# A build-time plan with measured durations, a lock for the score banks, six PSUM banks without fixed roles, and an earlier place for the mixing factors

## The chip, the cores and the metric

The kernel runs on one core of one Trainium2 chip. The metric is the device time of one execution in microseconds (us); the median of three runs stands for a kernel. The core has five engines that run side by side, each in the order of its own list: TensorE (PE, matmuls, with weight loads shown apart as PEld), VectorE (DVE), ScalarE (ACT), GpSimd (POOL), and SyncE (SP), which here issues all DMA transfers. They wait for one another by semaphores.

## The reference

Eight batches, eight heads, 576 tokens, head size 64. Each head's output is the sum of two attentions: one over queries, keys and values averaged over groups of four tokens, repeated four times, and a local one in which a token sees those less than four places away. The heads side by side give x, 8 x 576 x 512, which a channel-mixing layer takes:

```
q_d, k_d, v_d = mean over groups of 4 tokens
out = repeat(softmax(q_d k_d' / 8) v_d, 4) + softmax(mask(q k' / 8)) v
x_prev = x shifted by one token
xk = mu_k * x + (1 - mu_k) * x_prev
xr = mu_r * x + (1 - mu_r) * x_prev
k = relu(xk @ w_k)          # 512 -> 1024
v = (k * k) @ w_v           # 1024 -> 512
return sigmoid(xr @ w_r) * v
```

The three weight matrices arrive as 64-bit floats, so the kernel has to turn them into 32-bit numbers by bit operations.

## The kernel before

**Attention** goes by pairs of heads, 32 pairs (n), four to a batch. A pair's work is: load q and k (`load_raw`, tile raw, a ring of four), v in groups (`load_v4`, tile v or v4, a ring of two) and v in windows (`load_windows`, vw); transpose q and k on DVE (`turn_q`, `turn_k`); average on POOL (`pool_q`, `pool_k`, `pool_v`, L363 and L364); scores on PE into ps_a, two PSUM banks with the tag att; softmax on DVE, ACT and POOL (`down_top`, `score_top`, `down_exp`, `score_sub` and so on, among them `down_norm`, L485); transposes of the probabilities on PE (`down_turn`, L497 to L499) with a copy on ACT (`down_copy`, L506) and a spread on ACT (`spread`, L444); products with v on PE (`av_pe`, L516 and L522, into two banks pv, in the profile ps_v); and the sum of both outputs on DVE into xt (`av_out`, L555). From pair 5 on, the scores of a pair and the products of the pair before it are one step of PE (`run_pe`).

**The layer** goes by 18 chunks (c) of 256 tokens. A chunk needs: the difference of neighbouring tokens (`diff`, L576), the mixes (`mix_part`, L587 on ACT or L591 on DVE, with the mixing factors muk and mur; `mix_add`, `mix_high`, L605, `mix_low`, L610), eight products `k_pe` (L618, 12 matmuls each into a bank ps_g), relu and square on ACT (`k_relu`, L623; `k_high`, L629 and L630), a remainder (`k_low`, L637, on DVE or POOL), two products `r_pe` (L649, into ps_r), a sigmoid (`gate`, L658), eight steps `v_pe` (L667, accumulating in two banks acc), the last product (`store_mul`, L671) and the store. Every number is split in a high and a low part, so each product is three matmuls. Chunks 0 and 1 need batch 0; chunk 2 is the first that needs batch 1.

**The weights**: twenty tiles of 128 x 512, k0 to k7, v0 to v7 and r0 to r3, in the order k0-k3, v0-v3, k4-k7, v4-v7, r0-r3. Each is loaded on SP (`fetch_weight`, L223), written into a PSUM bank by ACT (`weight_scale`, L228), worked on by DVE three times (`weight_shift`, L232; `weight_tail`, L236; `weight_sign`, L241, into an SBUF tile w32, a ring of three shared with the gates), and its high part is taken by ACT (`weight_high`, L249). The low part of the first eight comes from PE through the same bank (`weight_diff`, L255 and L256) and ACT (`weight_left`, L259), and that of the others from POOL (`weight_low`, L264). By `w_bank(i)` the bank is c0 or c1 by turns.

**PSUM** has eight banks. Two are att. The other six have roles: g, a ring of two, for ps_g (and, for the first four pairs, the transposed probabilities, and ps_r of chunk 0); acc0 and acc1 for the accumulators, for ps_r of the later chunks, and for the products of the first four pairs; c0 and c1 for the weights and for the products of the later pairs.

**The order** of all work is set when the program is built. `Plan.add` records each step with its engine, an assumed duration in us, a rank (a due time), what it reads and writes, the ring slots that it takes (`new=`) and, for a load, an assumed DMA time. `Plan.order` then plays all engines forward by those numbers. Each time it takes the step that can start first, and the lowest rank among those that could start on that engine at the same moment. `SLACK` stretches the durations of all engines but PE, `SYNC` is the delay from one engine to another, and `PORT` lengthens some DVE steps while POOL works. A ring's slots are given in the order in which they were asked for, except for the tags in `ANY`. The order that comes out is emitted engine by engine and kept at run time, whatever the real durations are.

Of the kernel before, what the change touches and what calls it, by code (L numbers as in the profile page):

```python
# [17 lines left out]
P = 128  # L18
# [26 lines left out]
class Plan:  # L45
# [6 lines left out]
    ANY = ("c0", "c1", "sig")  # L52
    PORT = 0.6
    SYNC = 0.2
    SLACK = 1.06
# [33 lines left out]
    def order(self):  # L89
# [9 lines left out]
        free = {}  # L99
        dma_free = 0.0  # L100
# [6 lines left out]
        def start_of(t):  # L107
            s = max(ready_at[t["id"]], free.get(t["eng"], 0.0))
            for tile, tag in t["new"]:

# [11 lines left out]
        while waiting:  # L122
# [14 lines left out]
            s = starts[best]  # L137
            for tile, tag in t["new"]:
                ring[tag] = ring[tag][1:] + [tile]
                turn[tag] += 1  # L140
# [8 lines left out]
            end[best] = e  # L149
            self.when[best] = (s, s + us, e)  # L150
# [12 lines left out]
def attention_moe(ctx: ExitStack, tc, q, k, v, mu_k, mu_r, w_k, w_v, w_r, band, ident, out):  # L163
# [62 lines left out]
    def weight_scale(i):  # L226
        shaped[i] = pp.tile([P, 512], F32, tag=w_bank(i), name="ps_w", bufs=1)
        nc.scalar.activation(shaped[i], raws[i][:, :, 1].bitcast(F32), AF.Copy, scale=2.0 ** -112)  # L228
# [258 lines left out]
    def down_turn(n):  # L487

        d = st[n]
        if n < NP:  # L490
            d["ps_t"] = [pp.tile([72, 288], F32, tag="g", name="ps_t") for _ in range(2)]
# [16 lines left out]
    def av_pe(n):  # L508
# [4 lines left out]
        pv = [pp.tile([P, 432], F32, tag=x, name="ps_v", bufs=1) for x in av_banks(n)]  # L513
# [159 lines left out]
    def store_out(c, t):  # L673
# [5 lines left out]
                     xkl=2, xrh=1, xrl=1, kk=2, kh=4, kl=4, sig=3, g=2, acc0=1, acc1=1, c0=1, c1=1, att=1))  # L679
# [16 lines left out]
    def pair_loads(n):  # L696
        R, R1 = at_run[n], after(n)
        for nm in "qk":
            add("SP", 2.0, R - 18, load_raw, n, nm, new=[(f"{nm}raw{n}", "raw")], dma=1.92)
        add("SP", 0.5, R1 - 18, load_v4, n, new=[(f"v4{n}", "v4")], dma=1.26)  # L700
        add("SP", 2.0, R1 - 17, load_windows, n, new=[(f"vw{n}", "vw")], dma=1.92)

    def pair_scores(n, part):
        R, R1 = at_run[n], after(n)
        i = n % 2
        if part == 0:
            add("DVE", 0.78, R - 9, turn_q, n, r=[f"qraw{n}"], w=[f"qT{i}"])
            if SPLIT <= n < SPLIT + 2:
                add("POOL", 0.5, R - 9, clear_plane, i, w=[f"kT{i}"])
            add("DVE", 0.78 if n < SPLIT else 1.53, R - 8.5, turn_k, n, r=[f"kraw{n}"], w=[f"kT{i}"])  # L710
            add("POOL", 1.2, R - 7, pool_q, n, r=[f"qT{i}"], w=[f"qd.{i}"])
            add("ACT", 0.42, R - 6, last_q, n, w=[f"qd.{i}"])
            add("POOL", 1.4 if n < SPLIT else 2.0, R - 6, pool_k, n, r=[f"kT{i}"], new=[(f"kd{n}", "kd")])
            add(*(("DVE", 1.0) if n < VDVE else ("POOL", 2.15)), R1 - 8, pool_v, n, r=[f"v4{n}"], new=[(f"vd{n}", "vd")])
        if part == 1:
            add("DVE", 0.8, R1 - 14, down_top, n, r=[f"ps{n}"], w=[f"mxd{n}"])
            add("DVE", 1.12, R1 - 13.5, score_top, n, r=[f"ps{n}"], new=[(f"sm{n}", "sm")])
            add("ACT", 1.8, R1 - 13, down_exp, n, r=[f"ps{n}", f"mxd{n}"], new=[(f"ad{n}", "ad")])
            if n >= PEM:
                add("POOL", 0.92, R1 - 12, score_sub, n, w=[f"sm{n}"])  # L720
# [209 lines left out]
```

## Time and profile before

| | |
|---|---|
| time, median of 3 runs | 714.82 us (713.87 to 715.29) |
| the profiled execution, its time | 714.58 us |
| the profiled execution, its span | 712.8 us |
| mean granted TensorE clock | 0.964 of full speed |
| DMA | 62.19 MB, mean 87 GB/s |

The span runs from the first to the last record of the profile; the time counts what lies around it, too. "Busy" counts the time in which an engine has an instruction under way; issuing a DMA is not counted as busy. A row of the timeline gives start, duration, engine, line, operation, output<-inputs, count, and in brackets the idle time just before with what ended it. A row of the groups gives count, busy us, mean ns, then the idle time before and its releasers. A row of the windows view gives, for a stretch of the span, its length, the busy us of PE, PEld, DVE, ACT and POOL with their counts (an engine without such work may be left out), then granted clock, DMA busy share and GB/s. A row of the chain of waits gives start, duration, and the work that the end of the span can be traced back to.

### The profile page before, as it was taken

The page shows a single profiled execution, that of the slowest core. Times are in us where ns is not written, and L with a number is a line of the kernel's source. Part 1 is how long each engine was busy: PE and PEld are TensorE (multiplying, and loading weights), DVE is VectorE, ACT ScalarE, POOL GpSimd, SP SyncE. Part 2 cuts the span into 40 slices and gives each one's busy share as a digit, 9 for nine tenths or more (in the row PEclk, how much of TensorE's full clock was granted, in tenths as well). Part 3 has the DMA queues.
Part 4 walks back from the last instruction along what each step waited for, and adds up shares of the span by engine and source line. Part 5 has one row for each costly group of instructions (what it writes and reads, how often), then busy time and mean ns, then how long its engine had stood idle before and what let it go on. Part 6 is the DMA issues. An engine that isn't in the chain of part 4 may idle for free.

```text
span 712.8 us, 18403 instructions
## 1 busy us (share of the span) xinstructions
PE 658.3 (92%) x7352; PEld 565.4 (79%) x7352; DVE 470.3 (66%) x855; ACT 438.7 (62%) x1095; POOL 300.2 (42%) x374
## 2 busy tenths in 40 slices
PE   3576768997999999999999999999999999999997
PEld 1353657785878888888888888888888888988986
DVE  3764999749766887588852797577867874464111
ACT  2544886665856857576665657676757675744442
POOL 5533689655554555444242265435554521000000
PEclk9677799997999999999999999999999999999999
DMA  7899886554435343424142173434351100000000
GB/s 144 175 207 269 205 144 99 103 98 111 95 63 124 74 103 74 102 49 90 48 107 52 40 136 74 103 73 95 65 120 40 53 2 32 1 30 30 0 31 30
DMA packets 221848, 62.19 MB, mean 87 GB/s; under 512 B 205122, under 2 KB 214594, under 8 KB 221762
## 3 DMA queue, kind: packets, MB, share of 16 engines
q1 hardware_dynamic: 221762, 61.01, 39.8%
q8 instruction: 58, 0.95, 0.6%
q14 instruction: 28, 0.23, 0.1%
HBM read 51.55 MB, written 9.44 MB: 86 GB/s over the span
## 4 chain that ended last, share of the span: by engine, by line
PE 76%; DVE 9%; SPq 6%; DMA 5%; ACT 1%; issue 1%; POOL 0%; DVEq 0%; ACTq 0%; POOLq 0%
PE ps_g L618 26%; PE acc L667 25%; PE ps_r L649 14%; SPq L276 4%; PE ps_v L522 3%; PE ps_a L390 3%; PE ps_v L516 2%; DMA muk<-in_moe_mu_k_dram 1%; DMA wk<-in_moe_w_k_dram 1%; DMA vw<-in_v_dram 1%; SPq L299 1%; DVE ps_w L236 1%; PE ps_a L457 1%; DMA qraw<-in_q_dram 1%; DVE ps_w L232 1%
## 5 line engine op out<-in xcount | busy, mean ns | idle before, releaser
L618 PE MATMUL ps_g<-xkh,wk 128*128 128x256 f32 x1152 | 229.8, 286 | 4.8 <-ACT kk L623 4.1
L618 PEld LDWEIGHTS ps_g<-xkh,wk 128*128 128x128 f32 x1152 | 187.5, 191 | 11.4 <-ACT kk L623 4.7
L667 PE MATMUL acc<-wv,kh 128*128 128x512 f32 x576 | 182.4, 398 | 0.0
L618 PE MATMUL ps_g<-xkl,wk 128*128 128x256 f32 x576 | 163.1, 283 | 1.3 <-DVE xkl L610 1.3
L637 DVE TENSOR_TENSOR kl<-kk,kh 128x256 fp32r<-128x256 f32 x119 | 66.6, 561 | 108.6 <-ACT kh L630 100.6
L623 ACT ACTIVATE kk<-ps_g 128x256 f32<-128x256 f32 x144 | 54.9, 382 | 105.6 <-PE ps_g L618 102.0
L667 PE MATMUL acc<-wv,kl 128*128 128x512 f32 x288 | 113.6, 394 | 3.3 <-POOL kl L637 3.3
L667 PEld LDWEIGHTS acc<-wv,kh 128*128 128x128 f32 x576 | 102.1, 190 | 17.0 <-issue 0.2
L618 PEld LDWEIGHTS ps_g<-xkl,wk 128*128 128x128 f32 x576 | 110.4, 192 | 5.0 <-DVE xkl L610 1.6
L649 PE MATMUL ps_r<-wr,xrh 128*128 128x512 f32 x288 | 89.9, 393 | 0.5 <-DVE sig L671 0.2
L667 PEld LDWEIGHTS acc<-wv,kl 128*128 128x128 f32 x288 | 54.5, 189 | 17.1 <-POOL kl L637 4.8
L418 POOL TENSOR_TENSOR sm<-sm,mx 128x384 f32<-128x384 f32 x28 | 28.7, 1025 | 83.6 <-DVE mx L413 72.2
L630 ACT ACTIVATE kh<-kk 128x256 fp32r<-128x256 f32 x144 | 60.2, 418 | 4.6
L629 ACT ACTIVATE kk<-kk 128x256 f32<-128x256 f32 x144 | 60.1, 418 | 4.4
L637 POOL TENSOR_TENSOR kl<-kk,kh 128x256 fp32r<-128x256 f32 x25 | 20.5, 820 | 99.4 <-PE acc L667 81.4
L649 PEld LDWEIGHTS ps_r<-wr,xrh 128*128 128x128 f32 x288 | 52.3, 188 | 10.8 <-DVE sig L671 0.6
L464 DVE TENSOR_REDUCE mxd<-ps_a 128x3 f32<-128x432 f32 x32 | 19.4, 605 | 61.1 <-PE ps_a L390 54.2
L649 PE MATMUL ps_r<-wr,xrl 128*128 128x512 f32 x144 | 56.2, 390 | 0.0
L474 ACT ACTIVATE ad<-ps_a,mxd 128x144 f32<-128x144 f32 x96 | 35.4, 378 | 32.2 <-DVE mxd L465 12.1
L363 POOL TENSOR_TENSOR v<-v 72x512 f32<-72x512 f32 x32 | 45.5, 1421 | 20.7 <-DMA v<-in_v_dram 20.6
L364 POOL TENSOR_TENSOR vd<-v 72x256 f32<-72x256 f32 x32 | 24.3, 759 | 65.8 <-PE ps_v L516 64.5
L354 POOL TENSOR_TENSOR tk<-kz 64x288 f32<-64x288 f32 (+1 forms) x56 | 43.1, 771 | 10.6 <-DVE kz L327 5.4
(103 smaller groups left out, 1174.0 us busy)
## 6 DMA issues: line engine op xcount, KB each, us to landing
vw<-in_v_dram SPq DMA_DIRECT2D x126, 96.0 KB
qraw<-in_q_dram SPq DMA_DIRECT2D x128, 72.0 KB
kraw<-in_k_dram SPq DMA_DIRECT2D x128, 72.0 KB
v<-in_v_dram SPq DMA_DIRECT2D x32, 288.0 KB
out_dram<-sig SPq DMA_DIRECT2D x36, 256.0 KB
wk<-in_moe_w_k_dram SPq DMA_DIRECT2D x8, 512.0 KB
wv<-in_moe_w_v_dram SPq DMA_DIRECT2D x8, 512.0 KB
wr<-in_moe_w_r_dram SPq DMA_DIRECT2D x4, 512.0 KB
```

The source lines that it names most:

```text
L276: nc.sync.dma_start(raw[o:o + 32], src[b, 2 * p + e].rearrange("(c t) (g d) -> t c g d", t=32, g=2)[:, :, dh, :])
L354: nc.gpsimd.tensor_tensor(out=tk[h], in0=k4[:, :, 0:2], in1=k4[:, :, 2:4], op=ALU.add)
L363: eng.tensor_tensor(out=v4[:, :, 0:128], in0=v4[:, :, 0:128], in1=v4[:, :, 128:256], op=ALU.add)
L418: nc.gpsimd.tensor_tensor(out=s3, in0=s3, in1=mx[:, :, None].broadcast_to([P, 12, 32]), op=ALU.subtract)
L474: nc.scalar.activation(ad[:, t, :], ps[:, t, :], AF.Exp, scale=1.0 / 128, bias=mx[:, t:t + 1], accum_out=sd[:, t:t + 1])
L618: nc.tensor.matmul(ps, w_k_part(p, f, w), y[:, p, :], start=(m == 0), stop=(m == len(mm) - 1))
L623: nc.scalar.activation(kk, kq[c, f], AF.Relu)
L629: nc.scalar.activation(kk, kk, AF.Square)
L630: nc.scalar.activation(kh, kk, AF.Copy)
L637: eng.tensor_tensor(out=kl, in0=kk, in1=kh.bitcast(F32), op=ALU.subtract)
L649: nc.tensor.matmul(ps, y[:, p, P * t:P * t + P], ws[f"r{p}"][:, w, :], start=(m == 0), stop=(m == len(mm) - 1))
L667: nc.tensor.matmul(accs[c][t], x[:, P * t:P * t + P], ws[f"v{f}"][:, w, :], start=(f == 0 and m == 0), stop=(f == NF - 1 and m == 2))
```

## The change

No step of the computation is added or removed; its order, its PSUM banks and the plan's numbers are altered.

- The tags g, acc0, acc1, c0 and c1 go. Everything that used them asks for a "bank". `banks_for` gives one of six: among those whose last user has ended by the time at which the step could start, the ones freed latest; if there are too few, those that come free first. The chosen names b0 to b5 are kept in `plan.bank` and used as the tile's tag. att stays as it is.
- Three readers of a pair's score bank, `down_top`, `score_top` and `down_exp`, get a lock: in the plan, one starts only when the one before it has ended.
- The assumed durations are replaced; `SLACK` goes from 1.06 to 1.0, `SYNC` from 0.2 to 0.1, `PORT` from 0.6 to 0.8.
- `load_mus` goes from rank W0 = -25 to rank -88 and gets a DMA time of 0.8.

```
-    ANY = ("c0", "c1", "sig")
-    PORT = 0.6
-    SYNC = 0.2
-    SLACK = 1.06
+    ANY = ("sig",)
+    BANKS = 6
+    PORT = 0.8
+    SYNC = 0.1
+    SLACK = 1.0
...
+        def banks_for(t):
+            want = [tile for tile, tag in t["new"] if tag == "bank"]
+            if not want:
+                return 0.0, {}
+            s0 = max(ready_at[t["id"]], free.get(t["eng"], 0.0))
+            at = []
+            for k, old in enumerate(banks):
+                ends = [end.get(u) for u in self.tile_users[old]] if old is not None else []
+                if None not in ends:
+                    at.append((max(ends, default=-1.0) + self.SYNC, k))
+            if len(at) < len(want):
+                return None
+            late = sorted((x for x in at if x[0] <= s0), reverse=True)[:len(want)]
+            pick = late + sorted(x for x in at if x not in late)[:len(want) - len(late)]
+            return max(x[0] for x in pick), dict(zip(want, (k for _, k in pick)))
...
         def start_of(t):
-            s = max(ready_at[t["id"]], free.get(t["eng"], 0.0))
+            s = max(ready_at[t["id"]], free.get(t["eng"], 0.0), held.get(t["lock"], 0.0))
+            got = banks_for(t)
+            if got is None:
+                return None
+            s = max(s, got[0])
...
             end[best] = e
+            if t["lock"]:
+                held[t["lock"]] = e + self.SYNC
...
-        shaped[i] = pp.tile([P, 512], F32, tag=w_bank(i), name="ps_w", bufs=1)
+        shaped[i] = pp.tile([P, 512], F32, tag=plan.bank[f"ws{i}"], name="ps_w", bufs=1)
...
-        ps = pp.tile([P, CT], F32, tag="g", name="ps_g")
+        ps = pp.tile([P, CT], F32, tag=plan.bank[f"g{c}.{f}"], name="ps_g", bufs=1)
...
-            add("SP", 2.0, R - 18, load_raw, n, nm, new=[(f"{nm}raw{n}", "raw")], dma=1.92)
-        add("SP", 0.5, R1 - 18, load_v4, n, new=[(f"v4{n}", "v4")], dma=1.26)
-        add("SP", 2.0, R1 - 17, load_windows, n, new=[(f"vw{n}", "vw")], dma=1.92)
+            add("SP", 2.0, R - 18, load_raw, n, nm, new=[(f"{nm}raw{n}", "raw")], dma=2.4)
+        add("SP", 0.5, R1 - 18, load_v4, n, new=[(f"v4{n}", "v4")], dma=1.56)
+        add("SP", 2.0, R1 - 17, load_windows, n, new=[(f"vw{n}", "vw")], dma=2.5)
...
-            add("DVE", 0.8, R1 - 14, down_top, n, r=[f"ps{n}"], w=[f"mxd{n}"])
-            add("DVE", 1.12, R1 - 13.5, score_top, n, r=[f"ps{n}"], new=[(f"sm{n}", "sm")])
-            add("ACT", 1.8, R1 - 13, down_exp, n, r=[f"ps{n}", f"mxd{n}"], new=[(f"ad{n}", "ad")])
+            add("DVE", 0.8, R1 - 14, down_top, n, r=[f"ps{n}"], w=[f"mxd{n}"], lock=f"ps{n}")
+            add("DVE", 1.1, R1 - 13.5, score_top, n, r=[f"ps{n}"], new=[(f"sm{n}", "sm")], lock=f"ps{n}")
+            add("ACT", 1.2, R1 - 13, down_exp, n, r=[f"ps{n}", f"mxd{n}"], new=[(f"ad{n}", "ad")], lock=f"ps{n}")
...
         add("SP", 0.5, FETCH[i], fetch_weight, i, w=[base], dma=1.75)
-        add("ACT", 0.67, R, weight_scale, i, r=[base], new=[(f"ws{i}", w_bank(i))])
-        add("DVE", 0.6, R + 0.5, weight_shift, i, w=[f"ws{i}"])
+        add("ACT", 0.63, R, weight_scale, i, r=[base], new=[(f"ws{i}", "bank")])
+        add("DVE", 0.68, R + 0.5, weight_shift, i, w=[f"ws{i}"])
...
-        add("POOL", 2.2, -110, clear, w=["kT0", "kT1", "qT0", "qT1", "qd.0", "qd.1", "bd"])
-        add("SP", 1.0, W0, load_mus, w=["mu"])
+        add("POOL", 4.2, -110, clear, w=["kT0", "kT1", "qT0", "qT1", "qd.0", "qd.1", "bd"])
+        add("SP", 1.0, -88.0, load_mus, w=["mu"], dma=0.8)
```

More of the change, by code (lines that the diff above doesn't have):

```diff
@@ L99, in order @@
         free = {}
+        held = {}
+        banks, self.bank = [None] * self.BANKS, {}
+        def banks_for(t):
[13 more added lines that the diff above has]
+            return max(x[0] for x in pick), dict(zip(want, (k for _, k in pick)))
         dma_free = 0.0
@@ L137, in order @@
             s = starts[best]
+            for tile, k in banks_for(t)[1].items():
+                banks[k], self.bank[tile] = tile, f"b{k}"
             for tile, tag in t["new"]:
-                ring[tag] = ring[tag][1:] + [tile]
-                turn[tag] += 1
+                if tag != "bank":
+                    ring[tag] = ring[tag][1:] + [tile]
+                    turn[tag] += 1
             us = t["us"] * (1.0 if eng == "PE" else self.SLACK)
@@ L490, in down_turn @@
         if n < NP:
-            d["ps_t"] = [pp.tile([72, 288], F32, tag="g", name="ps_t") for _ in range(2)]
+            d["ps_t"] = [pp.tile([72, 288], F32, tag=plan.bank[f"pst{n}{kt}"], name="ps_t", bufs=1) for kt in range(2)]
         else:
@@ L512, in av_pe @@
         d = st[n]
-        pv = [pp.tile([P, 432], F32, tag=x, name="ps_v", bufs=1) for x in av_banks(n)]
+        pv = [pp.tile([P, 432], F32, tag=plan.bank[f"pv{n}{x}"], name="ps_v", bufs=1) for x in ("", "b")]
         for kt in range(2):
@@ L644, in r_pe @@
         xh, xl = xs[c, "xr"]
-        tag = r_bank(c, t)
-        ps = pp.tile([P, 512], F32, tag=tag, name="ps_r", bufs=2 if tag == "g" else 1)
+        ps = pp.tile([P, 512], F32, tag=plan.bank[f"r{c}.{t}"], name="ps_r", bufs=1)
         mm = [(y, w, p) for p in range(NP) for y, w in ((xh, 0), (xh, 1), (xl, 0))]
@@ L662, in v_pe @@
         if f == 0:
-            accs[c] = [pp.tile([P, 512], F32, tag=f"acc{t}", name=f"acc{t}", bufs=1) for t in range(2)]
+            accs[c] = [pp.tile([P, 512], F32, tag=plan.bank[f"acc{c}.{t}"], name=f"acc{t}", bufs=1) for t in range(2)]
         kh, kl = kq[c, f]
@@ L728, in pair_scores @@
+            add("DVE", 0.57, R1 - 6, score_turn, n, r=[f"sm{n}"], new=[(f"at{n}", "at")])
+            add("ACT", 0.95, R1 - 4, spread, n, r=[f"at{n}"], w=["bd"])
             add("PE", 0.65, R1 - 7, down_turn, n, r=[f"ad{n}"],
-                new=[(f"pst{n}{kt}", "g") for kt in range(2)] if n < NP else [(f"pst{n}0", "att")])
-            add("ACT", 0.85, R1 - 6, down_copy, n, r=[f"pst{n}0"] + ([f"pst{n}1"] if n < NP else []),
+                new=[(f"pst{n}{kt}", "bank") for kt in range(2)] if n < NP else [(f"pst{n}0", "att")])
@@ L807, in r_part @@
                 add("PE", 2.79, where[f"r{t}"], r_pe, c, t,
-                    r=[f"xrh{c}", f"xrl{c}"] + both(f"r{p}" for p in range(NP)), new=[(f"r{c}.{t}", r_bank(c, t))])
+                    r=[f"xrh{c}", f"xrl{c}"] + both(f"r{p}" for p in range(NP)), new=[(f"r{c}.{t}", "bank")])
             add("ACT", 3.8, where["r1"] - 3, gate, c, r=[f"r{c}.0", f"r{c}.1"],
@@ L814, in v_part @@
                 add("PE", 1.4, where[f"v{f}"], v_pe, c, f, r=[f"kh{c}.{f}", f"kl{c}.{f}"] + both([f"v{f}"]),
-                    new=[(f"acc{c}.{t}", f"acc{t}") for t in range(2)] if f == 0 else [],
+                    new=[(f"acc{c}.{t}", "bank") for t in range(2)] if f == 0 else [],
                     w=[f"acc{c}.{t}" for t in range(2)] if f else [])
```

74 lines of the change are left out of this document (34 added, 40 removed).

## The prediction

> **What bounds the kernel now.** I read the page first, for the share of each engine, and then the windows view, cut where the slices of the page change.
>
> ```profile
> span 712.8 us, 18403 instructions
> ...
> PE 658.3 (92%) x7352; PEld 565.4 (79%) x7352; DVE 470.3 (66%) x855; ACT 438.7 (62%) x1095; POOL 300.2 (42%) x374
> ```
>
> ```profile
> 10.00:74.00 64.00, 40.58 (x721) 25.95 (x721) 41.18 (x83) 31.38 (x84) 23.76 (x30) 0.74 0.95 206
> 74.00:128.00 54.00, 43.67 (x491) 36.73 (x492) 52.23 (x73) 39.72 (x100) 45.23 (x48) 0.92 0.76 148
> 128.00:175.00 47.00, 41.47 (x670) 34.07 (x672) 30.94 (x60) 30.34 (x79) 25.21 (x34) 0.92 0.50 102
> 175.00:210.00 35.00, 33.62 (x396) 29.50 (x392) 26.80 (x51) 23.31 (x58) 22.52 (x25) 0.96 0.42 81
> 210.00:709.00 499.00, 498.90 (x5099) 439.17 (x5089) 316.80 (x587) 311.94 (x772) 176.32 (x217) 1.00 0.28 63
> ```
>
> The profiled execution took 714.58 us, 1.8 more than its span of 712.8 and 0.2 below the median of 714.82, so no correction is needed. The windows rows (length, then busy time of PE, its weight loads, DVE, ACT, POOL, then clock and DMA) divide it into stages. From 210 to 709 PE is busy 498.90 of 499.00 us at a clock of 1.00. The same matmuls remain after the change, so here there is nothing to gain; the stage can only get worse. All that a better order can win lies before 210.
>
> From 10 to 74 the DMA engines are busy 0.95 of the time while four pairs of heads and sixteen of the twenty weight tiles come in. PE is busy 40.58 of 64.00 us at a clock of 0.74. DVE works only 41.18 us, so it idles 22.8. From 74 to 128 DVE is the bound: 52.23 of 54.00 us, 97%, while PE loses 10.33. From 128 to 175 PE loses 5.53 more, and 1.38 up to 210. PE idle from 74 to 210 is thus 10.33 + 5.53 + 1.38 = 17.2 us. That is the pool for an order that only fills PE, apart from an earlier start of chunk 0.
>
> What does DVE do in its full stage?
>
> ```profile
> 10.00:74.00 64.00, 14.72 (x24) 4.94 (x24) 17.11 (x26) 9.90 (x16) 0.74 0.95 206
> 74.00:128.00 54.00, 0.00 (x0) 0.00 (x0) 23.38 (x35) 7.42 (x12) 0.92 0.76 148
> ```
>
> ```profile
> L232 DVE TENSOR_SCALAR ps_w<-ps_w 128x512 int32<-128x512 int32 x20 | 13.7, 684 | 9.4 <-ACT ps_w L228 9.4
> L236 DVE SCALAR_TENSOR_TENSOR ps_w<-wk,ps_w 128x512 int32<-128x512 int32 x8 | 5.5, 689 | 0.2
> L241 DVE SCALAR_TENSOR_TENSOR w<-wk,ps_w 128x512 int32<-128x512 int32 x8 | 5.4, 674 | 0.2
> ```
>
> Instructions on the weight tile ps_w take 23.38 of those 52.23 us. One weight costs 0.684 + 0.689 + 0.674 = 2.05 us of DVE (shift, tail, sign), so about eleven and a half of the twenty conversions fall into the stage that DVE bounds, after a stage in which it idled 22.8 us. The ACT timeline (start, duration, what) shows why they come so late:
>
> ```profile
> 62.16 0.60 ACT L259 ACTIVATE wv<-ps_w 128x512 fp32r<-128x512 f32 x1 [0.87 <-PE ps_w L256]
> ...
> 63.18 0.63 ACT L228 ACTIVATE ps_w<-wv 128x512 f32<-128x512 f32 x1
> ...
> 64.94 0.60 ACT L259 ACTIVATE wv<-ps_w 128x512 fp32r<-128x512 f32 x1 [0.93 <-PE ps_w L256]
> ...
> 65.57 0.64 ACT L228 ACTIVATE ps_w<-wv 128x512 f32<-128x512 f32 x1
> ...
> 69.56 1.70 ACT L587 ACTIVATE xk<-dx,muk 128x256 f32<-128x256 f32 x4 [2.31 <-DMA muk<-in_moe_mu_k_dram]
> 71.17 0.57 ACT L259 ACTIVATE wv<-ps_w 128x512 fp32r<-128x512 f32 x1
> ...
> 72.17 0.62 ACT L228 ACTIVATE ps_w<-wk 128x512 f32<-128x512 f32 x1
> ...
> 75.27 0.57 ACT L259 ACTIVATE wv<-ps_w 128x512 fp32r<-128x512 f32 x1
> ...
> 76.20 0.65 ACT L228 ACTIVATE ps_w<-wk 128x512 f32<-128x512 f32 x1
> ```
>
> L228 begins a weight by writing its bank, c0 or c1 by turns; L259 is the last reader of that bank for the first eight weights. Four times a beginning (63.18, 65.57, 72.17, 76.20) follows the last read of the weight two before it (62.16, 64.94, 71.17, 75.27) within 1.1 us of its start. The last two are the fifth and sixth k tile. That their data had not just come, the chain of waits tells:
>
> ```profile
> 49.81 9.59 DMA wk<-in_moe_w_k_dram
> 59.42 10.05 DMA muk<-in_moe_mu_k_dram
> ```
>
> The first of the four later k tiles landed at 49.81 + 9.59 = 59.40, yet was begun at 72.17, 12.8 us later. The mixing factor, issued behind those k tiles and the last v tiles, landed at 69.47, so all eight were in by then (an inference from the order of issue).
>
> **The change, part by part.**
>
> *Six banks without roles.* It adds no instruction; it takes away the two-bank limit on weights, the two-bank ring of ps_g, and the sharing of acc between ps_r and the next accumulation. For weights the next limits are the landing and the ring of three w32 tiles. What room has DVE between 56 and 72?
>
> ```profile
> 59.35 0.58 DVE L438 STREAM_TRANSPOSE at<-sm 128x384 f32<-128x384 f32 x1 [3.39 <-POOL sm L433]
> ...
> 63.84 0.70 DVE L232 TENSOR_SCALAR ps_w<-ps_w 128x512 int32<-128x512 int32 x1 [2.61 <-ACT ps_w L228]
> ...
> 71.30 1.23 DVE L601 TENSOR_TENSOR xk<-xk,xt 128x1024 f32<-128x1024 f32 x1 [2.65 <-ACT xk L587]
> ```
>
> The idle times in brackets give 3.39 + 2.61 + 2.65 = 8.65 us; four weights need 4 x 2.05 = 8.2. So the four later k tiles fit there, beside waits for DMA and for pair 3. Taken out of the stage that DVE bounds at 97%, they bring the work behind them (turns, mixes and softmax of pairs 4 to 7, which chunk 2 needs) forward by up to 8.2 us, and PE has 17.2 us of idle time to give it back from. Bounds: nothing if the moved work meets another wait, and 17.2 if the whole pool goes. I take 8.2. The ring of ps_g itself has this row (whole waits in the stage, count, longest):
>
> ```profile
> PE ps_g L618 <- ACT kk L623: 4.1, 3, 1.7
> ```
>
> Its 4.1 us are part of the 17.2, not a sum beside it.
>
> *Mixing factors early.* Rank -25 becomes -88, which by the ranks puts both issues on SP ahead of the v tile of pair 1, the raw tiles of pairs 2 and 3 and everything up to the last v weight.
>
> ```profile
> 20.94 0.40 SPq L285 DMA_DIRECT2D v<-in_v_dram  x1
> ...
> 45.26 0.32 SPq L285 DMA_DIRECT2D v<-in_v_dram  x1
> ...
> 59.42 0.85 SPq L188 DMA_DIRECT2D muk<-in_moe_mu_k_dram  x1
> 61.21 0.37 SPq L189 DMA_DIRECT2D mur<-in_moe_mu_r_dram  x1
> 62.53 7.08 SPq L276 DMA_DIRECT2D qraw<-in_q_dram  x4
> ...
> 66.07 1.90 POOL L576 TENSOR_TENSOR dx<-xt 128x1024 f32<-128x1024 f32 x1 [6.76 <-DVE xt L555]
> ```
>
> The difference dx of chunk 0 ended at 66.07 + 1.90 = 67.97 and the first mix (L587, above) began at 69.56: 1.6 us go, if nothing else is late; next are the mixes themselves, in line on ACT. The price: the two issues hold SP 0.85 + 0.37 = 1.2 us, 3.1 with the gaps up to 62.53, and they are about 1024 packets of four bytes. The queue row prices a packet:
>
> ```profile
> q1 hardware_dynamic: 221762, 61.01, 39.8%
> ```
>
> 39.8% of 16 x 712.8 us over 221762 packets is 20.5 ns, so 1024 packets on 16 engines take about 1.3 us (estimate; the mean packet is 275 bytes, and smaller ones may be cheaper or dearer). DMA is full there, so v of pair 3, which POOL waits for, comes 1.3 us later (0 to 3.1). In return the raw tiles of pair 4 no longer stand behind them. Beside this row, the Trainium skill, DMA: Bandwidth & Descriptors (Measured), puts a small transfer at about 10.5 ns a packet and sets 512 B as the least for full rate (Specifications). By its price the 1.3 would be 0.7 us, an estimate; no row here isolates a four-byte packet.
>
> *Durations and lock.* They alter only the order. The lock keeps three readers of the score bank apart in the plan. The loads are re-rated from 1.92 to 2.4 us a raw tile, and so on. Adding the plan's own DMA terms up to v of pair 3 gives a planned landing near 45 us before (3 + 15.4 + 5.0 + 5.8 + 14 + 1.5) and near 52 after (3 + 19.2 + 6.2 + 7.5 + 14 + 0.8 + 1.5). The trace:
>
> ```profile
> 55.60 1.26 POOL L363 TENSOR_TENSOR v<-v 72x512 f32<-72x512 f32 x1 [6.58 <-DMA v<-in_v_dram]
> 56.94 0.72 POOL L364 TENSOR_TENSOR vd<-v 72x256 f32<-72x256 f32 x1
> 57.62 0.91 POOL L485 TENSOR_TENSOR ad<-ad,sd 128x432 f32<-128x432 f32 x1
> ...
> 58.58 0.43 PE L497 MATMUL ps_t<-idn,ad 128*72 128x128 f32 x1 [4.18 <-POOL ad L485]
> ...
> 62.70 0.91 PE L522 MATMUL ps_v<-bd,vw 64*64 64x48 f32 x48
> ...
> 73.82 0.58 PE L618 MATMUL ps_g<-xkh,wk 128*128 128x256 f32 x1 [0.70 <-ACT xkh L605]
> ```
>
> POOL stood 6.58 us at the head of its queue for v, with the normalisation of pair 3 (L485) behind it, and PE's transposes behind that. With L485 first, the sums behind it (vd ready at 57.66, against ps_v L522 at 62.70) could end up to 5.0 us earlier. With a plan still 3.4 us early the same order may stand, or a new one may wait as long elsewhere. Bounds -5.0 to +3.4; I take 0, since two of the three pool operations stay tied to that landing.
>
> *Less slack.* SLACK 1.06 becomes 1.0, SYNC 0.2 becomes 0.1, and a bank is picked as the latest freed before the start, with the least room. Where the plan is early by a little, PE now waits. PE falls behind the plan once and the others then have room, so I take 1.0 us; bounds 0 and 15 (one wait of the kind of L618 above, 4.1 / 3 = 1.4 us, in eleven of the chunks).
>
> Sum: 714.6 - 8.2 - 1.6 + 1.3 + 0 + 1.0 = 707.1, so 707 us.
>
> **Rivals.**
>
> 1. *The whole pool goes* (chance 0.15). If pairs 4 to 7 come early enough that chunk 2 never waits, all 17.2 us go, and the start gains 1.6 to 5: 714.6 - 17.2 - 1.6 = 695.8. For it: idle time of DVE in the first stage is 22.8 us, more than I use. Against it: DMA is at 0.95 there, and 0.76 even up to 128.
>
> 2. *A weight that has not landed stands at the head of ACT* (0.22), ending slower. Today the two banks hold weights back until long after landing. Without them the plan starts a weight where it believes its data to be. Its terms give a landing of the fifth k tile near 56.5 (52.2 + one vw of 2.5 + 1.75) against 59.40 in the trace, 2.9 us early. ACT and DVE are in order, so the exponentials, copies and spreads of pair 3 queue behind L228, and PE, POOL and chunk 0 behind those. Price: 3.4 us of start (the same error at v of pair 3) and 1.3 of packets, with none of the 8.2 recovered, because the DVE gaps of 59 to 72 then move with pair 3: 714.6 + 3.4 + 1.3 = 719.3. It decides once L228 of the fifth k tile stands on ACT ahead of L506 or L444 of pair 3. For it: in-order POOL already shows this very wait (6.58). Against it: later weights are planned nearly right.
>
> 3. *The steady stage loses what the start wins* (0.15): latest-freed banks and no slack cost PE about half a us in each of fourteen chunks, 7.5 in all: 707.1 + 7.5 - 1.0 = 713.6. Against it: PE idles 0.10 us in 499 with only two ps_g banks in turn. The Trainium skill, TensorE: The Clock Gate (A second HAM failure mode: psum-queue depth-cycling), says that cycling through PSUM banks can make PE idle briefly so often that its clock oscillates; the trace so far disagrees, with a clock of 1.00 in that stage. The rows give this a price too: at the 0.74 of the first stage, 20 us of steady work would take 27, again 7 us; no more of it is likely.
>
> **How the numbers follow.** My forecast, 707 with its own range of 701 to 712, has 0.48; the rivals 0.15, 0.22 and 0.15. A measurement of this kernel can tell about 0.2% (1.4 us) from no change. Faster: 0.48 + 0.15 + a third of rival 3 = 0.68. Same: half of rival 3, 0.08. Slower: 0.22 + the rest = 0.24. The range reaches from 696 (half of rival 1) to 719 (half of rival 2), leaving out about 0.17.
>
> **What would show it.** Right: L228 of the fifth k tile begins at 60 to 66, not 72.17; ps_w takes about 15 us of DVE after chunk 0 has begun, not 23.4; PE idle between 74 and 210 falls from 17 to 9; the first L618 starts within 2 us of 73.8; the window after 210 stays full. Wrong: ACT or DVE waits for a wk or v load of over 3 us between 45 and 70 with pair 3 behind it; PE waits for kk, pv or acc banks after 210; a clock under 1.00 there; or DVE just as full and the pairs as late, which would mean that the banks were not what held the weights back.

## The result, and the profile after

The changed kernel takes 706.69 us (median of 4 runs, 705.81 to 708.59), the kernel before 714.51 beside it (4 runs). The ratio is 0.9891 with a 95% interval of 0.9872 to 0.9911: 7.8 us less, where 7.8 was forecast (714.8 to 707.0).

The profiled execution took 708.59 us, the longest of the four, 1.9 above the median; its terms are therefore compared with one another more safely than with the median. First the head of the page, as for the kernel before:

```profile
span 706.7 us, 18406 instructions
...
PE 655.3 (93%) x7352; PEld 562.3 (80%) x7352; DVE 466.6 (66%) x855; ACT 438.9 (62%) x1095; POOL 303.1 (43%) x374
```

Then the windows view with the same stages:

```profile
10.00:74.00 64.00, 40.55 (x720) 26.73 (x720) 48.44 (x92) 35.96 (x92) 27.79 (x34) 0.74 0.95 208
74.00:128.00 54.00, 45.10 (x637) 38.94 (x638) 45.78 (x73) 35.46 (x95) 46.78 (x52) 0.90 0.90 156
128.00:175.00 47.00, 44.23 (x609) 37.81 (x608) 32.97 (x63) 36.23 (x92) 27.05 (x32) 1.00 0.52 107
175.00:210.00 35.00, 34.75 (x404) 29.69 (x403) 28.32 (x53) 21.91 (x56) 18.32 (x23) 1.00 0.42 92
210.00:702.00 492.00, 489.67 (x4985) 428.71 (x4984) 308.08 (x573) 307.31 (x758) 176.19 (x214) 1.00 0.30 62
```

The third number of a row after its length is DVE. It rises from 41.18 to 48.44 us in the first stage and falls from 52.23 to 45.78 in the second, so DVE is no longer the bound there. The idle time of PE is the length less the first number: 8.90, 2.77 and 0.25 us, together 11.9 from 74 to 210 in place of 17.2. After 210 it is 2.33, where it was 0.10.

The windows of the weight tile ps_w alone (PE, PEld, DVE, ACT), cut at the first matmul of chunk 0, show which work moved:

```profile
10.00:76.31 66.31, 13.83 (x24) 5.18 (x24) 26.31 (x39) 13.13 (x22) 0.73 0.95 212
76.31:128.00 51.69, 0.00 (x0) 0.00 (x0) 14.23 (x21) 3.71 (x6) 0.92 0.89 148
```

14.23 us of DVE work on weights are left behind that point; before it was 23.38 from 74 on. The ACT timeline shows the four later k tiles being begun:

```profile
62.57 0.63 ACT L258 ACTIVATE ps_w<-wk 128x512 f32<-128x512 f32 x1
...
64.14 0.62 ACT L258 ACTIVATE ps_w<-wk 128x512 f32<-128x512 f32 x1
...
64.87 0.61 ACT L258 ACTIVATE ps_w<-wk 128x512 f32<-128x512 f32 x1
...
66.50 0.62 ACT L258 ACTIVATE ps_w<-wk 128x512 f32<-128x512 f32 x1
```

L258 is the L228 of before. The fifth k tile begins at 62.57 instead of 72.17, and all four have begun by 66.50. But the start of chunk 0 did not come sooner. The DVE timeline up to it, and below it PE's:

```profile
71.69 0.69 DVE L271 SCALAR_TENSOR_TENSOR w<-wk,ps_w 128x512 int32<-128x512 int32 x1
72.29 1.74 DVE L625 TENSOR_TENSOR xk<-xk,xt 128x1024 f32<-128x1024 f32 x1
73.96 0.69 DVE L262 TENSOR_SCALAR ps_w<-ps_w 128x512 int32<-128x512 int32 x1
74.68 0.70 DVE L266 SCALAR_TENSOR_TENSOR ps_w<-wv,ps_w 128x512 int32<-128x512 int32 x1
75.48 0.69 DVE L271 SCALAR_TENSOR_TENSOR w<-wv,ps_w 128x512 int32<-128x512 int32 x1
76.08 1.22 DVE L634 TENSOR_TENSOR xkl<-xk,xkh 128x1024 fp32r<-128x1024 f32 x1
```

```profile
76.31 0.55 PE L642 MATMUL ps_g<-xkh,wk 128*128 128x256 f32 x1 [11.25 <-DVE w L271]
77.36 0.58 PE L642 MATMUL ps_g<-xkl,wk 128*128 128x256 f32 x1 [0.49 <-DVE xkl L634]
```

The sum of the mix (L625) stands in DVE's list behind a k weight's sign pass, and the low part of the mix (L634) behind three passes of a v weight. The first matmul waits for a bank which that v weight holds until L271 has read it (75.48 + 0.69 = 76.17). So it starts at 76.31, 2.5 us later than before.

The span can be taken apart into the start of the first `k_pe`, PE's idle time after it, and PE's busy time after it. The last is the page's PE total less the busy time up to that start, 658.3 - 40.4 before and 655.3 - 40.55 after.

| profiled execution | start of chunk 0 | PE idle after | PE busy after | span |
|---|---|---|---|---|
| before | 73.8 | 21.1 | 617.9 | 712.8 |
| changed | 76.3 | 15.7 | 614.7 | 706.7 |
| difference | +2.5 | -5.4 | -3.2 | -6.1 |

The -5.4 are -7.6 up to 210 us and +2.2 after it: from its own start of chunk 0 to 210, PE is idle 17.2 us before and 9.6 in the changed kernel. (The 11.9 above also hold the 2.3 us from 74 to the late start.)

The same matmuls are busy for 3.2 us less, and for a part of that time their clock is higher: from 128 to 175 us it is 1.00, where it was 0.92. That the clock accounts for all of it is not shown: old_margins, below, is busy 614.2 us after its start with a clock of 0.85 in that stage.

### The profile page after: what moved, and what is told of

Its sections match the earlier page's. It is cut to its first block, busy times and chain, and to the rows that moved or that the text cites. A ratio compares the mean times of both kernels' runs of the same rounds, so it can differ in the third digit from the quotient of the medians.

```text
span 706.7 us, 18406 instructions
## 1 busy us (share of the span) xinstructions
PE 655.3 (93%) x7352; PEld 562.3 (80%) x7352; DVE 466.6 (66%) x855; ACT 438.9 (62%) x1095; POOL 303.1 (43%) x374
## 4 chain that ended last, share of the span: by engine, by line
PE 73%; DVE 11%; POOL 5%; ACT 4%; issue 3%; SPq 2%; DMA 2%; DVEq 0%; POOLq 0%; ACTq 0%
PE ps_g L642 24%; PE acc L687 22%; PE ps_r L672 12%; PE ps_v L549 3%; PE ps_a L417 2%; PE ps_v L543 2%; SPq L303 1%; PE ps_a L477 1%; PE ps_a L484 1%; ACT L501 1%; ACT ad L501 1%; DVE mxd L491 1%; PE ps_a L422 1%; DVE kl L661 1%; PE ps_t L524 1%
## 5 line engine op out<-in xcount | busy, mean ns | idle before, releaser
L642 PE MATMUL ps_g<-xkh,wk 128*128 128x256 f32 x1152 | 230.1, 286 | 14.2 <-DVE w L271 11.9
L661 DVE TENSOR_TENSOR kl<-kk,kh 128x256 fp32r<-128x256 f32 x119 | 64.2, 540 | 118.0 <-ACT kh L654 110.8
L647 ACT ACTIVATE kk<-ps_g 128x256 f32<-128x256 f32 x144 | 54.5, 379 | 84.8 <-PE ps_g L642 79.1
L661 POOL TENSOR_TENSOR kl<-kk,kh 128x256 fp32r<-128x256 f32 x25 | 18.5, 740 | 125.0 <-PE acc L687 96.1
L445 POOL TENSOR_TENSOR sm<-sm,mx 128x384 f32<-128x384 f32 x28 | 24.3, 866 | 83.1 <-DVE sd L507 60.7
L390 POOL TENSOR_TENSOR v<-v 72x512 f32<-72x512 f32 x32 | 44.6, 1395 | 12.4 <-DMA v<-in_v_dram 12.3
L391 POOL TENSOR_TENSOR vd<-v 72x256 f32<-72x256 f32 x32 | 27.7, 866 | 51.0 <-PE ps_v L543 49.6
L381 POOL TENSOR_TENSOR tk<-kz 64x288 f32<-64x288 f32 (+1 forms) x56 | 40.9, 731 | 16.5 <-DVE kz L354 12.5
```

What stands on the lines that cost most here:

```text
L381: nc.gpsimd.tensor_tensor(out=tk[h], in0=k4[:, :, 0:2], in1=k4[:, :, 2:4], op=ALU.add)
L390: eng.tensor_tensor(out=v4[:, :, 0:128], in0=v4[:, :, 0:128], in1=v4[:, :, 128:256], op=ALU.add)
L391: eng.tensor_tensor(out=vd, in0=v4[:, :, 0:64], in1=v4[:, :, 64:128], op=ALU.add)
L642: nc.tensor.matmul(ps, w_k_part(p, f, w), y[:, p, :], start=(m == 0), stop=(m == len(mm) - 1))
L647: nc.scalar.activation(kk, kq[c, f], AF.Relu)
L661: eng.tensor_tensor(out=kl, in0=kk, in1=kh.bitcast(F32), op=ALU.subtract)
```

## The experiments

Twelve kernels, timed against the kernel before on the same chip. In each the result is the median; the ratio is to the kernel before. That kernel's medians beside them, 714.33 to 714.48 us, hardly differ, so medians of different groups of runs, on different chips, are compared here, too. Starts, idle times and busy times are those of the one profiled execution of a kernel. Where a plan's number or rule is edited the plan is made anew, and with it the order on all engines, except where the text says otherwise.

### One part alone, on the kernel before

**banks_only**: six banks with latest-freed choice; every number, margin and rank as before, no lock.

```
-    ANY = ("c0", "c1", "sig")
+    ANY = ("sig",)
+    BANKS = 6
...
+        def banks_for(t):
...
-        ps = pp.tile([P, CT], F32, tag="g", name="ps_g")
+        ps = pp.tile([P, CT], F32, tag=plan.bank[f"g{c}.{f}"], name="ps_g", bufs=1)
```

> Only the six banks without roles; the durations, SLACK, SYNC, PORT, no lock and the late mixing factors are those of before. Theory 1 (the banks win by letting weights be converted before chunk 0): 705 to 709 us, the scaling of the fifth k tile begins at 60 to 66 us as it does in the changed kernel (62.6) and not at 72.2, and PE is idle about 12 us between 74 and 210, not 17. Theory 2 (the measured durations win, the banks only go along): 713 to 716 us, with the old idle time of PE.

Measured: 715.69 us, 1.0014 [1.0002, 1.0026]. The part that was to bring 8.2 us brings nothing by itself. Its weights do move (the fifth k tile is begun at 62.10, as theory 1 asked), as the windows of ps_w show, cut at its own first `k_pe`:

```profile
10.00:83.18 73.18, 13.38 (x24) 5.29 (x24) 28.15 (x42) 15.94 (x26) 0.73 0.98 215
83.18:128.00 44.82, 0.00 (x0) 0.00 (x0) 12.25 (x18) 1.23 (x2) 0.90 0.79 129
```

Only 12.25 us of DVE work on weights are left behind that start. But the start itself is at 83.18, 9.4 us later than before. PE's idle time after it is 15.0 us (21.1 before), so the late start takes back what the fuller stage gives. The waits of PE between 74 and 210 (total, times, longest) list banks held by others at the top:

```profile
PE ps_g L642 <- DVE w L271: 5.4, 1, 5.4
PE ps_g L642 <- ACT sig L678: 3.9, 1, 3.9
```

**banks_oldest**: the same, but the bank that has been free longest.

```
-            late = sorted((x for x in at if x[0] <= s0), reverse=True)[:len(want)]
-            pick = late + sorted(x for x in at if x not in late)[:len(want) - len(late)]
+            pick = sorted(at)[:len(want)]
```

> The six banks alone, as in banks_only (old durations, margins and DMA times, no lock, late mixing factors), but a plan that takes the bank that has been free longest. Theory 1 (banks_only gained nothing because its late weights and chunk 0 wait for one another's banks: it lists 5.4 us behind the weights' DVE pass and 3.9 us behind the sigmoids): most of that goes, first k matmul before 78 us and 706 to 711 us. Theory 2 (it gained nothing because the old DMA times let the plan hand work to engines before its data has landed, and because early weights crowd chunk 0): first k matmul stays behind 80 us and the time stays at 712 to 717 us.

Measured: 713.69 us, 0.9992 [0.9979, 1.0006], first `k_pe` at 81.11. That is what theory 2 gave and not theory 1: six banks alone gain nothing that can be measured, and chunk 0 starts 7 to 9 us late under both rules of choice. The plan finds the same order on all five engines as for banks_only, so the two differ only in the banks: the wait of 5.4 us behind the weight's pass is gone, the one behind the sigmoids is still 3.3, chunk 0 starts 2.1 us sooner, and the median is 2.0 us lower, though the two intervals overlap. Which of theory 2's two grounds it is, the DMA times or the crowd of weights, this run doesn't tell.

**numbers_only**: durations, margins, DMA times and lock of the change; the roles of the banks and the rank of the mixing factors as before.

```
-    SLACK = 1.06
+    SLACK = 1.0
...
-            add("SP", 2.0, R - 18, load_raw, n, nm, new=[(f"{nm}raw{n}", "raw")], dma=1.92)
+            add("SP", 2.0, R - 18, load_raw, n, nm, new=[(f"{nm}raw{n}", "raw")], dma=2.4)
...
```

> Only the new durations, SLACK, SYNC, PORT and the lock, with the old roles of the banks and the late mixing factors. Theory 1: 713 to 717 us, the fifth k tile still begun at 70 us or later, because two banks hold it back. Theory 2: 705 to 709 us. If both parts are needed together, both this run and the one with the banks alone stay above 711.

Measured: 712.99 us, 0.9981 [0.9966, 0.9996]: 1.5 us less, at the edge of theory 1. Both this run and banks_only stay above 711, as the expectation said if both parts are needed together. But theory 1's reason is only half right. With two banks the fifth k tile is begun long before 70 us; the two behind it wait until 70.70:

```profile
62.06 0.65 ACT L231 ACTIVATE ps_w<-wk 128x512 f32<-128x512 f32 x1
...
70.70 1.16 ACT L231 ACTIVATE ps_w<-wk 128x512 f32<-128x512 f32 x2
```

**factors_only**: the kernel before with the mixing factors fetched early.

```
-        add("SP", 1.0, W0, load_mus, w=["mu"])
+        add("SP", 1.0, -88.0, load_mus, w=["mu"], dma=0.8)
```

> Only the mixing factors' rank and DMA time. The recorded working gave -1.6 us for the wait and +1.3 for the packets ahead of v of pair 3: 714 to 715, no change that can be told. A rival: the two issues cost SP so much that chunk 0 starts later: 716 to 718. Another: the wait was hiding a longer one and all later loads come 3 us earlier: 711 to 713.

Measured: 710.21 us, 0.9932 [0.9905, 0.9959]: 4.3 us less, with chunk 0 at 73.9, no earlier than before. That is outside all three ranges given, and its runs are far apart (706.64 to 712.03, the last being the profiled one). The gain is in PE's idle time after the start (17.6 us for 21.1), where the prediction had put none of it. Its cause stays open.

The three parts alone, +1.2, -1.5 and -4.3 us, make -4.6 together; the change makes -7.8. They don't add, but the 3.2 us between the two sums are less than the scatter of orders found below.

### One part undone, in the changed kernel

**factors_late**: the mixing factors at their old rank.

```
-        add("SP", 1.0, -88.0, load_mus, w=["mu"], dma=0.8)
+        add("SP", 1.0, W0, load_mus, w=["mu"])
```

> The changed kernel with the mixing factors back at their late rank and without a DMA time. If their place is worth nothing there, 706 to 708 us. If chunk 0 of the changed kernel would have to wait for them (they landed at 69.5 us before, and its first mix begins at 69.4 now), at most 1 us more: 706.5 to 708.5. If they are a pillar of the gain: 710 or more.

Measured: 706.79 us, 0.9886 [0.9859, 0.9913], against 0.9891 of the changed kernel. Inside the change the early fetch is worth nothing measurable. On PE, DVE, ACT and POOL the two plans differ in 17 places only, so this is nearly a comparison within one order.

**two_weight_banks**: at most two weights in PSUM at a time, the limit of before, by a ring of two that holds no memory.

```
...
-        add("ACT", 0.63, R, weight_scale, i, r=[base], new=[(f"ws{i}", "bank")])
+        add("ACT", 0.63, R, weight_scale, i, r=[base], new=[(f"ws{i}", "bank"), (f"wb{i}", "wb")])
...
```

> The changed kernel, with at most two weights at a time in PSUM, in any of the six banks, so that weights wait for the second weight before them as they did before the change. All else keeps its freedom. Theory 1 as recorded (weights converted early are what the banks win): 712 to 715 us, idle time of PE after its first layer product back from 16 to about 20 us. Theory 3, formed after the runs of the parts (early weights win idle time of PE later and lose it again at the start of chunk 0, which they delay by 2.5 us in the changed kernel and by 9.4 with the old durations): chunk 0 starts at 73 to 75 instead of 76.3 us, 2 us earlier, idle time after it is 4 us longer, so 708 to 711 us. If the weights do not matter at all: 705 to 708 us.

Measured: 709.85 us, 0.9942 [0.9929, 0.9955]: 3.2 us of the change are lost when weights may no longer run ahead, not 8.2. The time is in theory 3's range. Chunk 0 starts at 74.39, as it said, but PE's idle time after that is 17.3 us, 1.7 longer than the 15.6 of the changed kernel and not 4; its busy time is 618.0, 3.2 longer. From the start to 210 us PE is idle 10.8 us (changed 9.6, before 17.2). So under the two-bank limit, with another order, most of the fall in idle time is still there.

**old_margins**: `SLACK`, `SYNC` and `PORT` as before.

```
-    PORT = 0.8
-    SYNC = 0.1
-    SLACK = 1.0
+    PORT = 0.6
+    SYNC = 0.2
+    SLACK = 1.06
```

> The changed kernel with SLACK 1.06, SYNC 0.2 and PORT 0.6 as before. My term of +1.0 us for the smaller margins: 705 to 706 us, with the idle time after 210 us down from 2.3 to 0.1. Rival (the margins are part of a good start, since a slower plan orders other things first): chunk 0 at 79 us or later and 708 to 712 us.

Measured: 711.24 us, 0.996 [0.9944, 0.9976]: 4.5 us slower than the change. The number is the rival's, but its reason isn't: chunk 0 starts at 72.64, sooner than in the changed kernel. After 210 us the idle time does fall, to 0.85. The loss lies from 128 to 175 us:

```profile
128.00:175.00 47.00, 35.04 (x537) 29.95 (x536) 31.54 (x58) 24.75 (x63) 22.57 (x29) 0.85 0.41 89
```

PE is idle 11.96 us there (the changed kernel 2.77), for the most part behind POOL's normalisation (L512, 5.7 us) and a mix (6.0).

**old_dma_times**: DMA times of raw, v and vw as before.

```
-            add("SP", 2.0, R - 18, load_raw, n, nm, new=[(f"{nm}raw{n}", "raw")], dma=2.4)
+            add("SP", 2.0, R - 18, load_raw, n, nm, new=[(f"{nm}raw{n}", "raw")], dma=1.92)
...
```

> The changed kernel with the old DMA times of raw, v and vw tiles (1.92, 1.26, 1.92) in the plan. Theory 3 (the measured DMA times keep weights and pair 3 from being put at the head of a queue before their data is there): chunk 0 starts at 80 us or later, ACT or DVE stands over 3 us before a weight or behind v, 709 to 714 us. Rival (DMA times do not matter, the engine durations do): 705 to 708 us, start near 76 us.

Measured: 718.23 us, 1.0053 [1.0034, 1.0071]: 11.5 us slower than the change and slower than before, outside both ranges. Chunk 0 starts at 73.9, not at 80 or later, and from 45 to 76 us ACT's longest wait for a weight is 2.2. The wait that the prediction found on POOL is back, longer. POOL's waits from 10 to 76 us, then its timeline there, then that of the changed kernel:

```profile
POOL v L390 <- DMA v<-in_v_dram: 21.7, 4, 7.8
```

```profile
54.60 1.27 POOL L390 TENSOR_TENSOR v<-v 72x512 f32<-72x512 f32 x1 [7.85 <-DMA v<-in_v_dram]
55.95 0.73 POOL L391 TENSOR_TENSOR vd<-v 72x256 f32<-72x256 f32 x1
56.64 0.90 POOL L512 TENSOR_TENSOR ad<-ad,sd 128x432 f32<-128x432 f32 x1
```

```profile
56.64 0.91 POOL L512 TENSOR_TENSOR ad<-ad,sd 128x432 f32<-128x432 f32 x1 [8.87 <-DVE sd L508]
57.50 1.27 POOL L390 TENSOR_TENSOR v<-v 72x512 f32<-72x512 f32 x1
```

The re-rating does put the normalisation of pair 3 (L512, the L485 of before) ahead of the pooling of v (L390). Yet it begins at 56.64 in both: with the wait for v gone, it waits 8.87 us for its sums from DVE instead. So the 11.5 us do not come from this place; and with PE idle 21.8 us after a start of 73.9, and busy 617.9, its profiled execution is like that of the kernel before in every term of the table. That execution took 715.47 us, 2.8 below the median, so the profile holds only a part of the 11.5.

**no_lock**: without the lock.

```
...
-            add("ACT", 1.2, R1 - 13, down_exp, n, r=[f"ps{n}", f"mxd{n}"], new=[(f"ad{n}", "ad")], lock=f"ps{n}")
+            add("ACT", 1.2, R1 - 13, down_exp, n, r=[f"ps{n}", f"mxd{n}"], new=[(f"ad{n}", "ad")])
...
```

> The change without the lock alone. Theory 1 (the lock does nothing for the path, as the prediction had it; the readers of one score bank are in its order on DVE anyway): 705 to 709 us. Theory 2 (it keeps the exponential off the head of ACT's queue, where it would hold the conversions behind it): 710 to 714 us, with more idle of PE between 74 and 210 us than the 12.0 us of the changed kernel.

Measured: 717.53 us, 1.0049 [1.0031, 1.0066], outside what either theory gave. Theory 1 falls as a number; theory 2 has the direction, but little of the size: from 74 to 210 us PE is idle 13.6 us (the changed kernel 11.9), and from 45 to 76 us the exponential stands idle at the head of ACT once, for 1.55 us. Chunk 0 starts at 72.96, sooner than with the lock. From 210 to 702 us PE is idle 5.55 us (the changed kernel 2.33):

```profile
210.00:702.00 492.00, 486.45 (x4961) 424.68 (x4960) 307.16 (x572) 305.49 (x750) 173.90 (x212) 1.00 0.29 63
```

After its start PE is idle 23.4 us in all and busy 619.1 (changed 15.6 and 614.7). Why a plan without the lock comes out so is not shown.

### The same order, other banks

**oldest_bank**: the changed kernel with the bank that has been free longest, the edit shown under banks_oldest. Here the plan finds the same order of instructions on all five engines as for the changed kernel; only the bank behind a tile differs. With banks_only and banks_oldest it is one of the two pairs in this study that aren't also a comparison of two orders.

> The changed kernel, giving the bank that has been free longest instead of the one freed last. Theory (the first layer product waits 1.2 us for a bank that a weight still holds, and the 2.3 us of idle time of PE after 210 us are such waits): start of chunk 0 at about 75.1 us, under 0.5 us of idle time after 210, 703 to 705 us. Rival (the waits are for data, the bank only shows in the semaphore): 706 to 708 us, nothing moved.

Measured: 703.29 us (702.02 to 703.74), 0.9842 [0.983, 0.9855]; the interval does not touch that of the changed kernel. The choice of the latest-freed bank costs 3.4 us. PE's waits of the changed kernel from 210 to 702 us, and the windows row of oldest_bank for that stage, up to its last matmuls:

```profile
PE ps_g L642 <- ACT kk L647: 2.0, 3, 0.8
PE ps_g L642 <- DVE xt L579: 0.2, 1, 0.2
```

```profile
210.00:695.00 485.00, 484.91 (x4962) 426.00 (x4961) 304.44 (x567) 304.06 (x754) 172.32 (x209) 1.00 0.30 62
```

Four times PE stands before a bank whose last reader has just ended by the plan but not in fact: three times the relu (L647), once the sum xt. With the bank free longest none of it is left: 0.09 us idle of 485. It takes the small margins as well: with the same choice of bank and the old margins, old_margins waits 0.2 us for such banks after 210, and banks_only lists none. At chunk 0 the bank held by the v weight no longer counts either:

```profile
74.04 0.58 PE L641 MATMUL ps_g<-xkh,wk 128*128 128x256 f32 x1 [10.16 <-ACT xkh L628]
76.22 0.58 PE L641 MATMUL ps_g<-xkl,wk 128*128 128x256 f32 x1 [1.60 <-DVE xkl L633]
```

(Lines stand one lower in this kernel.) The first matmul goes when its data is there, but the second still waits for the low part, so of the 2.3 us at the first only 77.36 - 76.22 = 1.1 carry on, and DVE ran about a us earlier in this execution anyway (by 1.0 from 54 us on; the sum of the mix began at 71.16, not 72.29). The profiled spans differ by 6.7 us, more than the medians; the 2.2 us of the steady stage are the part that the rows tie to the banks. This is the fastest version of the study, faster than both kernels.

### How much of it is the luck of an order

**nudge_shift**: one assumed duration off by a hundredth of a us.

```
-            add("DVE", 0.68, R + 0.5, weight_shift, i, w=[f"ws{i}"])
+            add("DVE", 0.69, R + 0.5, weight_shift, i, w=[f"ws{i}"])
```

> The change with one duration that it measured nudged by a hundredth: 0.69 for 0.68 us of the weights' shift. No mechanism is touched; only the order that the plan finds can move. Theory 1 (plans of the same rules give the same time): 706 to 707.5 us. Theory 2 (the order is a matter of luck by some us, so that differences between other re-planned kernels mean little under that size): outside 704 to 709.5 us.

Measured: 710.63 us (709.09 to 711.39), 0.9943 [0.9928, 0.9958]: 3.9 us slower than the change, as theory 2 said. Up to the start of chunk 0 the plan's order and its banks are those of the changed kernel. Yet the start is at 78.09, not 76.31: so far apart can two executions of the same plan be there. A difference of under 2 us between the starts of two profiles shows nothing by itself.

**nudge_oldest**: oldest_bank, with another duration off by a hundredth.

```
-            add("ACT", 0.82, W - 6, k_high, c, f, w=[f"kk{c}.{f}"], new=[(f"kh{c}.{f}", "kh")])
+            add("ACT", 0.81, W - 6, k_high, c, f, w=[f"kk{c}.{f}"], new=[(f"kh{c}.{f}", "kh")])
```

> The kernel with the bank free longest, and one duration nudged by a hundredth, 0.81 for 0.82 us of k_high, by which the plan finds another order over a large part of the program. Theory 1 (the gain of that bank rule comes from the waits that it spares, whatever the order): 701.5 to 705 us. Theory 2 (a re-plan scatters by more than that gain): above 706 us, the lost time as idle of PE between 10 and 210 us.

Measured: 712.71 us (710.15 to 713.8), 0.9971 [0.9959, 0.9984]: 9.4 us slower than oldest_bank, theory 2 again. The windows row from 128 to 175 us tells where most of it lies:

```profile
128.00:175.00 47.00, 40.30 (x550) 33.66 (x554) 28.27 (x58) 27.55 (x72) 25.46 (x33) 0.86 0.45 89
```

PE idles 6.70 us there (oldest_bank 1.43) at a clock of 0.86 (1.00). Over the whole program its idle time after chunk 0's start is 18.5 us and its busy time 618.6, against 13.0 and 613.0 of oldest_bank. From 210 on, though, it idles 0.09 us again: what the oldest bank spares in the steady stage holds under a second order, while the order of the first 200 us outweighs it.

So two plans of the same rules lie up to 9.4 us apart. That is the measure for all the experiments that re-plan: +3.2 (two_weight_banks), +4.5 (old_margins) and -4.3 (factors_only) are within it, and +11.5 (old_dma_times) and +10.8 (no_lock) are only just beyond the larger of two samples. None of these differences can be put down to the edited part alone. What stands beyond it: all three plans of the whole change that were timed (706.69, 706.79 with late factors, 710.63) are faster than before, and so is the one with the oldest bank under either order. The kernel before was not nudged: its 714.5 is one draw of its rules too, and how far it is an unlucky one is not known.

## Why the prediction was right, and where it was not

The time was right; its split was not.

**Banks, -8.2.** The mechanism was read rightly in part. Without the roles, four k tiles did go into DVE's idle time of 56 to 72 us, and the amount of moved work was right too (DVE +7.3 us in the first stage, -6.5 in the second, from the windows). But the two banks were not all that held the weights back. With two banks and another order the fifth k tile begins at 62.06 (numbers_only) or 64.64 (two_weight_banks), and only the two behind it wait until 70.70 or 71.35. In the kernel before, PE had finished with the fifth tile's bank by 67.31 + 0.70 = 68.01:

```profile
67.31 0.70 PE L256 MATMUL ps_w<-wv,nidn 128*128 128x512 f32 x1
```

Its last reader (L259 at 71.17, in the prediction) stood on ACT behind chunk 0's first mix, so ACT's order held that bank 3.2 us longer.

The step that failed is the next one, that the moved weights bring "the work behind them (turns, mixes and softmax of pairs 4 to 7, which chunk 2 needs) forward by up to 8.2 us" at no cost to the start of chunk 0. From that start to 210 us PE's idle time did fall by 7.6, near the 8.2. But the start gave 2.5 back, because weights now stand ahead of chunk 0's mixes on DVE and ACT and in its banks, and 3.2 us came as shorter busy time, which was no term of the sum at all. The prediction asked that the start stay within 2 us of 73.82; it was 76.31 (78.73 in factors_late and 78.09 in nudge_shift, against 73.90 in factors_only). That the 7.6 come from the moved weights is not shown either: two_weight_banks, whose weights are held back, keeps 6.5 of them. By themselves the banks gained nothing (banks_only, banks_oldest): the start went to 81 to 83 us.

**Mixing factors, -1.6 + 1.3.** Near nothing was predicted, and inside the change near nothing was found (factors_late). The wait for muk is gone, but the mix begins at 69.37 instead of 69.56: the sum xt that chunk 0's difference needs ends 0.8 us later (66.78 for 65.99), and on POOL the low part of a k weight now stands ahead of the difference, as its timeline shows:

```profile
66.19 1.29 POOL L291 TENSOR_TENSOR wk<-w,wk 128x512 fp32r<-128x512 f32 x1 [5.82 <-ACT wk L276]
67.43 1.91 POOL L600 TENSOR_TENSOR dx<-xt 128x1024 f32<-128x1024 f32 x1
```

The prediction named the mixes on ACT as next late; it was dx. The 1.3 us for packets was not isolated, nor the 0.7 beside it.

**Durations and lock, 0 within -5.0 to +3.4.** At the place that the bounds came from, 0 was right: L512 passed v and met another wait. That they "alter only the order" was the mistake of weight: a hundredth of a us in one duration alters the order by 3.9 us and by 9.4. The bounds were drawn from one wait; they should have come from the scatter of orders.

**Less slack and latest-freed banks, +1.0.** The direction was right, and the reason too: PE meets a bank that is free by the plan and not in fact. oldest_bank measures the choice at 3.4 us, so the term was a third of its size. What the reduced margins do to the time is not measured apart from the order; the waits after 210 us need them as well as the choice.

**Rivals.** Not the whole pool went: after the start of chunk 0, 9.6 of 17.2 us are still idle. No weight that had not landed stood at the head of ACT; its longest wait from 45 to 76 us is another:

```profile
ACT up L571 <- PE ps_v L549: 3.6, 1, 3.6
```

The steady stage did lose, but 2.2 us (2.33 idle for 0.10), not 7.5, and its clock stayed at 1.00 with six banks in turn. The rule on depth-cycling that the prediction cited from the Trainium skill, TensorE: Matmul & The Clock Gate (A second HAM failure mode: psum-queue depth-cycling), shows no effect in this trace either.

What stays open: how much of the 7.8 us belongs to each part. The nearest to an answer is that the change with its own order gains 7.8 and one nudged order of the same change 3.9. A sum that meets the median to 0.3 us was therefore partly luck.

## What to carry to other kernels

When a planner sets the order, an edit of one of its numbers is a draw from many orders: time two or three nudged plans before a difference of under about 10 us in 700 is put down to a mechanism, or look for a pair that keeps the order, as oldest_bank did. Where several buffers are free, take the one that has been free longest: with the order unchanged it saved 3.4 us here, since it leaves room for the planner's errors (and 2.0 in the other pair, at the edge of what can be told). Work that is moved into idle time ahead of a start should be priced at that start first, by the rows that stand before it on each engine.

## What the runs showed of the hardware

The same sum of a mix, 128 x 1024, took 1.23 us on DVE before (at 71.30, with POOL idle from 67.97 to 73.29) and 1.74 after (at 72.29), while POOL worked on a weight. POOL's own operation beside it, and the one before, of the same shape:

```profile
69.28 1.30 POOL L291 TENSOR_TENSOR wk<-w,wk 128x512 fp32r<-128x512 f32 x1
71.68 1.27 POOL L291 TENSOR_TENSOR wk<-w,wk 128x512 fp32r<-128x512 f32 x1 [1.09 <-ACT wk L276]
73.17 2.00 POOL L291 TENSOR_TENSOR wk<-w,wk 128x512 fp32r<-128x512 f32 x1 [0.23 <-ACT wk L276]
```

In each overlap the one that began second took longer. POOL's operation of 71.68 took its usual 1.27 us; the mix, begun at 72.29 beside it, ended 1.08 us after it (72.95, 74.03). POOL's next, begun at 73.17 beside the mix, took 2.00 us where its neighbours took 1.27 to 1.30, and ended 1.14 us after the mix (75.17). Alone they take 1.23 and 1.30 us, so each did little until the other had ended. The mix's second sum shows the same behind POOL's operation of 77.32, which ended at 78.62; it ended at 79.69:

```profile
77.32 1.30 POOL L291 TENSOR_TENSOR wv<-w,wv 128x512 fp32r<-128x512 f32 x1 [2.14 <-ACT wv L276]
```

```profile
77.91 1.78 DVE L625 TENSOR_TENSOR dx<-dx,xt 128x1024 f32<-128x1024 f32 x1
```

So weights brought forward slowed chunk 0's mix by half a us even where they don't stand ahead of it in its list.

In the pair before and after, the kernel with less idle time also ran the same matmuls in less busy time, 614.7 for 617.9 us, at a clock of 1.00 for 0.92 in one stage of 47 us. Whether the idle time is what lowers the clock, and at what price, is not shown: over all the profiled executions the two go together only loosely, and old_margins is idle 21.4 us after its start and busy only 614.2.
